# Moving one weight-block issue off ScalarE's queue, and three small reorderings in the head of a layernorm / gated-MLP / state-space kernel

## Chip, cores and metric

The kernel runs on one core of one Trainium2 chip. The metric is the device time of one execution in microseconds (us), as the median of several runs. A run counts as slow when it is over 1.5% above the fastest run of the same kernel; slow runs are named and left out of every comparison.

Engine names in the profile: PE is TensorE's matmuls, PEld its weight loads (they overlap PE: in the kernel before the two are busy for 94% and 47% of the span), DVE is VectorE, ACT is ScalarE, POOL is GpSimd, SP is SyncE. "ACTq" is ScalarE's instruction queue when it issues a DMA. L436 is line 436 of the kernel named; the same statement has another line number in another kernel. Below, "position 15.6" means 15.6 us after the start of the profiled span.

## The reference

The input x has 2048 tokens of 448 columns. It is normalized, and then used twice: by a diagonal complex state-space recurrence, and by a gated MLP of width 1792.

```python
xn = layernorm(x)                                   # x: 1 x 2048 x 448
# A: state-space part, 448 complex states
Lam_bar = exp(dt * Lam);  B_bar = ((Lam_bar - 1) / Lam)[:, None] * Bmat
Bu = einsum("bld,pd->blp", xn, B_bar)               # "projections"
h_t = Lam_bar * h_(t-1) + Bu_t                      # 2048 steps
s = 2 * Re(einsum("blp,dp->bld", h, Cmat)) + xn * Dskip
# B: gated MLP
u = xn @ w_up;  gate = sigmoid(xn @ w_gate)         # 448 x 1792 each
g = silu((gate * u) @ w_down)
return x + s * g
```

## The kernel before

TensorE does all matrix products; VectorE does the scans and half of the evacuations from PSUM; ScalarE does tanh (for the sigmoid), copies and SiLU. A small list scheduler in the Python program decides each engine's order: `add(engine, cost, function, r=reads, w=writes)` records an operation, and the costs serve the ordering alone. `chain=True` keeps operations of one engine in program order.

Only the first 20 us matter here. In this "head" the first four token tiles (128 tokens each) are normalized, transposed on TensorE, and fed to the first three gate column blocks, token by token (`g_head`, 128 columns per matmul). The fourth such step is followed by full gate steps of 512 columns. The normalization of these four tiles needs a square root on ScalarE.

```python
for t in range(4):
    load_x(t, 1, ("SP", "ACT")[t % 2])
load_w("SP", "g", 0, 0)                # (queue, gate/up, row half, block)
load_w("ACT", "g", 1, 0)
...                                    # four short parameter rows
add("ACT", 0.3, lambda: A.preload_act_table_set("sqrt_and_others"), ..., chain=True)
for b in (1, 2):
    load_w("SP", "g", 0, b)
    load_w("ACT", "g", 1, b)           # b == 2: the third block, half of it from ScalarE
load_x(4, 4)
for b in (0, 1):
    load_w("SP", "u", 0, b)
    load_w("SP", "u", 1, b)

def warm_mm(n):                        # matmuls on zeros, to keep TensorE busy
    def f():
        for _ in range(n):
            T.matmul(gu[2][:, 0, :], lhsT=warm[:, 0:P], rhs=warm[:], start=True, stop=True)
    add("PE", 0.43 * n, f, r=["warm"], w=[("gu", 2)])

def chain(t0, n): ...                  # for t0 < 4: sqrt on ACT, then reciprocal on DVE

def pe_transpose(t):                   # xn -> acc (PSUM) -> xnT
    ...
    if t == 0:
        ...                            # 4 blocks copied by ACT, 3 by DVE
    else:
        add("ACT", 0.8, lambda: A.copy(out=xnT[0][:, :, js], in_=tp[:, :, :]), ...)

def tables():                          # sine and cosine tables of the recurrence
    add("ACT", 1.3, lambda: A.preload_act_table_set("silu_and_others"),
        r=["r", "dt", ("xnT", 0, 3, "a")], w=["silutab"])
    ...

warm_mm(9)
for t in range(4):
    stats(t); chain(t, 1); norm(t)
pe_transpose(0); warm_mm(1); pe_transpose(1)
columns(); warm_mm(2); g_head(0, 1)    # columns(): parameter rows to columns
pe_transpose(2); g_head(1, 2)
pe_transpose(3); g_head(2, 3)
...                                    # last 128-column step, then 512-column gate steps
b_load()                               # transposed loads of B, then bT copied by DVE
```

After the head come seven gate and seven up column blocks of 512 tokens for the first chunk. Each gate block is evacuated by a tanh on ScalarE, each up block by a multiply on VectorE. After them come the projections of the state-space part.

Of the kernel before, what the change touches and what calls it, by code (L numbers as in the profile page):

```python
# [14 lines left out]
ACT = mybir.ActivationFunctionType  # L15
# [57 lines left out]
class Plan:  # L73
# [8 lines left out]
    def add(self, eng, cost, fn, r=(), w=(), dma=0, lat=None, chain=False, name=""):  # L82
        o = Op()
        o.idx, o.eng, o.cost, o.fn, o.dma, o.name = len(self.ops), eng, cost, fn, dma, name
        o.lat = LAT.get(eng, 0.0) if lat is None else lat
        o.pre, o.suc = {}, []
        o.start = o.end = None
        for k in r:
            if k in self.w:
                self._edge(self.w[k], o, True)  # L90
        for k in w:
            for q in self.r.get(k, ()):
                self._edge(q, o, False)
            if k in self.w:
                self._edge(self.w[k], o, True)
        for k in w:
            self.w[k] = o
            self.r[k] = []
        for k in r:
            if k not in w:  # L100
                self.r.setdefault(k, []).append(o)
        if chain or eng == "PE":
            key = ("chain", eng)
            if key in self.last_of:
                self._edge(self.last_of[key], o, None)
            self.last_of[key] = o
        self.ops.append(o)
        return o
# [23 lines left out]
    def solve(self, pe_from):  # L132
        t = 0.0
        late = {}
        for o in self.ops:
            if o.eng == "PE":
                t = max(t, pe_from.get(o.name, 0.0))
                late[o.idx] = t
                t += o.cost
        for o in self.ops:  # L140
            o.late = late.get(o.idx, self.horizon)
            for a, kind in o.pre.values():
                a.suc.append((o, kind))
        back = {}
        ready = {}
        for o in self.ops:
            o.left = len(o.suc)

        def release(o):
            end = o.late + o.cost if o.eng == "PE" else min(  # L150
                [self.horizon] + [b.late - self._gap(o, b, k) - self._margin(o, b, k) for b, k in o.suc])
            ready.setdefault(o.eng, []).append((end, o))
        for o in self.ops:
            if not o.left:
                release(o)
        todo = len(self.ops)
        while todo:
            best = None
            for e, lst in ready.items():
                if lst:  # L160
                    t = min(back.get(e, 1e9), max(x[0] for x in lst))
                    if best is None or t > best[0]:
                        best = (t, e)
            t, e = best
            lst = ready[e]
            if e == "PE":
                pick = max(lst, key=lambda x: x[1].idx)
            else:
                pick = max((x for x in lst if x[0] >= t - 1e-9), key=lambda x: (x[0], x[1].idx))
            lst.remove(pick)  # L170
            o = pick[1]
            if e == "NONE":
                o.late = pick[0]
            elif e != "PE":
                o.late = t - o.cost
                back[e] = o.late
            todo -= 1
            for a, kind in o.pre.values():
                a.left -= 1
                if not a.left:  # L180
                    release(a)
        free = {}
        avail = {}
        for o in self.ops:
            o.left = len(o.pre)
            if not o.left:
                avail.setdefault(o.eng, []).append((0.0, o))
        todo = len(self.ops)
        dma_free = {}
        while todo:  # L190
            best = None
            for e, lst in avail.items():
                if lst:
                    s = max(free.get(e, 0.0), min(x[0] for x in lst))
                    if best is None or s < best[0]:
                        best = (s, e)
            s, e = best
            lst = avail[e]
            pick = min((x for x in lst if x[0] <= s + 1e-9), key=lambda x: (x[1].late, x[1].idx))
            lst.remove(pick)  # L200
            o = pick[1]
            o.start, o.end = s, s + o.cost
            free[e] = o.end
            if o.dma:
                if e == "POOL":
                    o.lat = 8.0
                else:
                    q = dma_free[0] = max(dma_free.get(0, 0.0), o.end + 1.2) + o.dma / 280e3
                    o.lat = q + 0.6 - o.end
            todo -= 1  # L210
            for b, kind in o.suc:
                b.left -= 1
                if not b.left:
                    rd = max(a.end + self._gap(a, b, k) for a, k in b.pre.values())
                    avail.setdefault(b.eng, []).append((rd, b))
# [7 lines left out]
def kernel(  # L223
# [18 lines left out]
    V, A, G, T, Q = nc.vector, nc.scalar, nc.gpsimd, nc.tensor, nc.sync  # L242
# [23 lines left out]
    xnT = [flat(t[:], 7, L) for t in xnT_raw]  # L266
# [25 lines left out]
    warm = sbt("warm", [512])  # L292
# [23 lines left out]
    gu = [pp.tile([P, 2, 512], FP32, name=f"gu{i}") for i in range(3)]  # L316
    acc = [pp.tile([P, 512], FP32, name=f"acc{i}") for i in range(2)]

    pl = Plan(185.0)
    add = pl.add  # L320
# [14 lines left out]
    def load_w(eng, k, half, b, r=()):  # L335
        m0, m1 = BLK[k][b]
        ps = slice(half * H, half * H + H)
        c0 = half * 896
        load(eng, [("w", k, half, m) for m in range(m0, m1)], H * 7 * (m1 - m0) * P * 2,
             wgt[k][ps, :, m0 * P:m1 * P],  # L340
             wsrc[k][:, c0 + m0 * P:c0 + m1 * P].rearrange("(s p) f -> p s f", p=H), r=r)

    def tload(keys, o, i, nbytes, r=(), chain=True):
        add("SP", 1.2, lambda: Q.dma_start_transpose(out=o, in_=i), r=r, w=keys, dma=nbytes * 1.5, chain=chain)


    add("DVE", 0.2, lambda: V.memset(warm[:], 0.0), w=["warm"])
    add("POOL", 0.15, lambda: G.memset(ident[:], 0.0), w=["ident"])
    add("POOL", 0.4, lambda: G.affine_select(out=ident[:], in_=ident[:], compare_op=ALU.not_equal, fill=1.0, base=0,
                                             pattern=[[-1, P]], channel_multiplier=1), r=["ident"], w=["ident"])  # L350
# [5 lines left out]
    add("POOL", 0.6, lambda: G.iota(iota[:, 0:NTAB], pattern=[[1, NTAB]], base=0, channel_multiplier=0,  # L356
                                    allow_small_or_imprecise_dtypes=True), w=[("wv", 0)])

    for t in range(4):
        load_x(t, 1, ("SP", "ACT")[t % 2])  # L360
    load_w("SP", "g", 0, 0)
# [1 line left out]
    for k, vec in enumerate((A_log_dt, A_Lambda_im, A_Lambda_re, A_Dskip)):  # L363
        load("ACT" if k < 2 else "SP", ("vrow", k), D * 2, vrow[k:k + 1, :], vec.unsqueeze(0), cost=0.25)
    add("ACT", 0.3, lambda: A.preload_act_table_set("sqrt_and_others"), w=["sqrttab"], lat=1.0, chain=True)
    for b in (1, 2):
        load_w("SP", "g", 0, b)
        load_w("ACT", "g", 1, b)
    load_x(4, 4)
    for b in (0, 1):  # L370
        load_w("SP", "u", 0, b)
# [3 lines left out]
    def warm_mm(n):  # L375
        def f():
            for _ in range(n):
                T.matmul(gu[2][:, 0, :], lhsT=warm[:, 0:P], rhs=warm[:], start=True, stop=True)
        add("PE", 0.43 * n, f, r=["warm"], w=[("gu", 2)])


    def stats(t):
# [47 lines left out]
    def pe_transpose(t):  # L430
        b, a, js = t % NXN, next_acc(), slice(t * P, t * P + P)
        tp = flat(acc[a][:].bitcast(BF16)[:, 0:7 * P], 7, P)

        def f(s0, s1):
            for s in range(s0, s1):
                T.transpose(tp[:, s, :], xn[b][:, s * H:s * H + P], ident[:, :])  # L436
        add("PE", 0.36, lambda: f(0, 6), r=[("xn", b), "ident"], w=[("acc", a)])
        add("PE", 0.06, lambda: f(6, 7), r=[("xnw", b), ("xn", b), "ident", ("acc", a)], w=[("acc", a)])
        if t == 0:
            add("ACT", 0.476, lambda: A.copy(out=xnT[0][:, 0:4, js], in_=tp[:, 0:4, :]),  # L440
                r=[("acc", a)], w=[("xnT", 0, t, "a")])
            add("DVE", 0.27, lambda: V.tensor_copy(out=xnT[0][:, 4:7, js], in_=tp[:, 4:7, :]),
                r=[("acc", a)], w=[("xnT", 0, t, "b")])
        else:
            add("ACT", 0.8, lambda: A.copy(out=xnT[0][:, :, js], in_=tp[:, :, :]),
                r=[("acc", a)], w=[("xnT", 0, t, "a"), ("xnT", 0, t, "b")])

    def dma_transpose(t):
# [60 lines left out]

    def tables():  # L510
        turn = C("turn")
        add("ACT", 1.3, lambda: A.preload_act_table_set("silu_and_others"), r=["r", "dt", ("xnT", 0, 3, "a")], w=["silutab"])
        for pt in range(4):
            vk, nk = ("v", pt), ("nu", pt)
            v, nu = v_t[:, pt, :], nu_t[:, pt, :]
# [2 lines left out]
                r=[("wv", 0), "turn"], w=[vk])  # L518
            add("DVE", 0.4, lambda v=v, nu=nu: V.tensor_single_scalar(out=nu, in_=v, scalar=MAGIC, op=ALU.add),
                r=[vk], w=[nk])  # L520
            add("DVE", 0.6, lambda v=v, nu=nu: V.scalar_tensor_tensor(out=nu, in0=nu, scalar=-MAGIC, in1=v,
                                                                      op0=ALU.add, op1=ALU.subtract),
                r=[vk, nk], w=[nk])
            add("DVE", 0.344, lambda v=v, nu=nu: V.tensor_single_scalar(out=v.bitcast(I32), in_=nu.bitcast(I32),
                                                                        scalar=0x7FFFFFFF, op=ALU.bitwise_and),
                r=[nk], w=[vk])
            so, co = (spm[:, pt, 0, :], cosT[:, pt, :]) if pt < 3 else (cs3[:, 1, :], cs3[:, 0, :])
            add("ACT", 0.537, lambda so=so, nu=nu: A.activation(so, nu[:, 0:L], ACT.Sin, scale=-S),
                r=[nk, "silutab"], w=[("sin", pt)])
# [343 lines left out]
    def g_head(lo, hi):  # L873
        for m in range(3):
            gu_mm(0, "g", m, slots0[m], lo, hi, m == 0)

    pe_transpose(0)
    warm_mm(1)
    pe_transpose(1)
    columns()  # L880
    warm_mm(2)
    g_head(0, 1)
    pe_transpose(2)
    g_head(1, 2)
    pe_transpose(3)
# [139 lines left out]
```

## Time and profile before

The time was 199.57 us (median of 3 runs, 198.74 to 200.06). The profiled run's span was 197.5 us.

The first lines are from the profile's page of the kernel before: busy time of each engine with its share of the span and the number of instructions, and TensorE's granted clock in tenths over 40 equal slices of the span.

```profile
PE 186.0 (94%) x1483; PEld 93.5 (47%) x1490; DVE 161.1 (82%) x278; ACT 87.0 (44%) x122; POOL 36.7 (19%) x90
...
PEclk9959999999999999999999999999999999999999
```

TensorE is busy nearly everywhere. The third digit of the clock, 5, is the one stretch of the head in which half clock is recorded. (Nothing is recorded before 5.48. The nine warm-up matmuls there start 0.43 us apart, eleven matmuls of the same shape at 36.43 take 2.54 us together, and pairs of 512-column matmuls start every 0.22 us at 23 to 24, so the warm-up ran at half that rate too, though its digits say 9.) The table by windows of the kernel before shows it closer. Its columns are the window, its length, then busy time and instruction count of PE, PEld, DVE, ACT and POOL, the granted clock, the mean load of the DMA engines, and GB/s.

```profile
5.00:10.00 5.00, 1.88 (x22) 1.35 (x22) 2.60 (x9) 1.89 (x5) 0.67 (x3) 0.89 0.84 220
10.00:15.00 5.00, 5.00 (x71) 3.85 (x71) 3.92 (x15) 2.95 (x6) 4.53 (x11) 0.50 1.12 231
...
40.00:60.00 20.00, 19.66 (x148) 9.13 (x149) 19.91 (x31) 12.45 (x18) 0.00 (x0) 1.00 0.51 139
60.00:100.00 40.00, 39.41 (x296) 18.88 (x296) 39.31 (x69) 19.41 (x28) 12.24 (x18) 1.00 0.11 24
```

From 40 on, TensorE idles for 0.34 us in 20 and VectorE for 0.09. There, a change to the head cannot make anything shorter; it can only make it start sooner. In the head TensorE idles (1.88 of 5 us busy) and then runs at half clock.

The timeline of the kernel before shows why. Its columns are start, duration, engine, line, operation and operands, count, and in brackets the engine's idle time just before and what ended it.

```profile
3.60 1.28 ACT L365 ACT_TABLE_LOAD   x1 [3.60 <-DMA x_all<-in_A_x_dram]
3.65 3.06 ACTq L326 DMA_DIRECT2D wG<-in_B_w_gate_dram  x2
...
6.82 0.48 ACT L393 ACTIVATE sdb<-mv,epsc 128x1 bf16<-128x1 bf16 x2 [1.94 <-DMA wG<-in_B_w_gate_dram]
7.88 0.56 PE L436 MATMUL acc<-ident,xn 128*128 128x128 bf16 x7 [2.69 <-DVE xn L407]
...
19.96 0.37 PE L647 MATMUL gu<-xnT,wG 64*128 64x512 bf16 x1 [0.88 <-ACT hF L661]
...
21.44 0.37 PE L648 MATMUL gu<-xnT,wG 64*128 64x512 bf16 x1 [0.24 <-issue]
...
26.42 0.38 PE L647 MATMUL gu<-xnT,wU 64*128 64x512 bf16 x1
...
29.57 0.39 DVE L592 COPY bT<-bT 64x896 bf16<-64x896 bf16 x1
...
35.48 0.38 PE L686 MATMUL gu<-xnT,bT 64*128 64x512 bf16 x1
```

ScalarE's table is loaded at 4.88, but its first square root starts at 6.82. The bracket names what it waited for: a gate-weight DMA. ScalarE does not need the data. It is the issue of the third gate block (the second of the two in the ACTq line, 3.06 us together) that goes out only at 6.09, when the first block's transfer has landed (6.07), and in this trace nothing that stands behind it on ScalarE starts before it is out. In the trace the two transfers report their landing on the same semaphore, which may be why the one issue waits for the other transfer. The normalization and the first transpose come behind that, at 7.88. The line at 21.44 matters later: TensorE stopped for a moment and no semaphore explains it ("issue"). The last three lines are the first "up" matmul, the copy of B and the first projection matmul.

### The profile page before, as it was taken

The page shows a single profiled execution, that of the slowest core. Times are in us where ns is not written, and L with a number is a line of the kernel's source. Part 1 is how long each engine was busy: PE and PEld are TensorE (multiplying, and loading weights), DVE is VectorE, ACT ScalarE, POOL GpSimd, SP SyncE. Part 2 cuts the span into 40 slices and gives each one's busy share as a digit, 9 for nine tenths or more (in the row PEclk, how much of TensorE's full clock was granted, in tenths as well). Part 3 has the DMA queues.
Part 4 walks back from the last instruction along what each step waited for, and adds up shares of the span by engine and source line. Part 5 has one row for each costly group of instructions (what it writes and reads, how often), then busy time and mean ns, then how long its engine had stood idle before and what let it go on. Part 6 is the DMA issues. An engine that isn't in the chain of part 4 may idle for free.

```text
span 197.5 us, 3713 instructions
## 1 busy us (share of the span) xinstructions
PE 186.0 (94%) x1483; PEld 93.5 (47%) x1490; DVE 161.1 (82%) x278; ACT 87.0 (44%) x122; POOL 36.7 (19%) x90
## 2 busy tenths in 40 slices
PE   7398999999999999999999999999989999999992
PEld 2277455444445445543445444444435444455561
DVE  3579539699999989999999999999998999630043
ACT  2356898366749573224568221524335331210110
POOL 4186528000004770000257000000000000000000
PEclk9959999999999999999999999999999999999999
DMA  5899957498100014300016410000000000010002
GB/s 159 219 232 225 155 113 97 122 320 226 56 0 0 3 27 91 68 3 0 0 25 89 103 43 3 23 0 27 23 23 0 3 0 25 23 49 24 0 23 71
DMA packets 30025, 13.31 MB, mean 67 GB/s; under 512 B 19636, under 2 KB 30008, under 8 KB 30008
## 3 DMA queue, kind: packets, MB, share of 16 engines
q1 hardware_dynamic: 28324, 12.05, 28.0%
q10 hardware_dynamic: 1684, 1.03, 2.0%
q8 instruction: 11, 0.18, 0.4%
q14 instruction: 6, 0.05, 0.1%
HBM read 6.66 MB, written 1.84 MB: 43 GB/s over the span
## 4 chain that ended last, share of the span: by engine, by line
DVE 48%; PE 35%; issue 6%; POOL 3%; ACT 3%; DMA 2%; SPq 0%; ACTq 0%; DVEq 0%; POOLq 0%
DVE hF L664 10%; PE gu L647 9%; DVE wv L753 8%; PE gu L648 7%; PE acc L837 5%; PE gu L814 5%; PE acc L814 4%; DVE ta L746 3%; DVE tb L747 3%; DVE z L749 3%; DVE hT L770 2%; DMA wG<-in_B_w_gate_dram 2%; DVE ta L767 2%; DVE tb L768 2%; DVE o_t L850 2%
## 5 line engine op out<-in xcount | busy, mean ns | idle before, releaser
L647 PE MATMUL gu<-xnT,wG 64*128 64x512 bf16 (+1 forms) x259 | 48.6, 338 | 1.0 <-ACT hF L661 0.9
L648 PE MATMUL gu<-xnT,wG 64*128 64x512 bf16 (+1 forms) x259 | 48.6, 338 | 0.2 <-issue 0.2
L647 PE MATMUL gu<-xnT,wU 64*128 64x512 bf16 x196 | 46.1, 377 | 0.0
L648 PE MATMUL gu<-xnT,wU 64*128 64x512 bf16 x196 | 46.0, 376 | 0.0
L661 ACT ACTIVATE sig<-gu 128x1024 f32<-128x1024 f32 x21 | 21.4, 1021 | 37.3 <-PE gu L648 37.3
L814 PE MATMUL acc<-wd,hF 128*128 128x448 bf16 x168 | 33.8, 353 | 0.0
L647 PEld LDWEIGHTS <-wG 64*128 64x128 bf16 x259 | 22.4, 101 | 20.2 <-issue 3.1
L814 PEld LDWEIGHTS <-hF 128*128 128x128 bf16 x224 | 21.5, 98 | 21.4 <-issue 2.1
L647 PEld LDWEIGHTS <-wU 64*128 64x128 bf16 x196 | 18.0, 94 | 18.6 <-issue 2.1
L664 DVE SCALAR_TENSOR_TENSOR hF<-sig,gu 128x1024 bf16<-128x1024 f32 x21 | 25.2, 1206 | 0.8 <-PE gu L648 0.8
L837 PE MATMUL acc<-cT,hT 128*128 128x448 bf16 x105 | 24.3, 353 | 0.0
L648 PEld LDWEIGHTS <-wG 64*128 64x128 bf16 x259 | 22.4, 101 | 3.4 <-issue 1.2
L753 DVE TENSOR_TENSOR_SCAN wv<-c_r,st,z 128x512 bf16<-128x512 f32 x18 | 22.8, 1273 | 0.0
L850 DVE TENSOR_TENSOR o_t<-acc,g_t 128x448 bf16<-128x448 f32 x15 | 9.2, 615 | 16.0 <-PE acc L837 16.0
L648 PEld LDWEIGHTS <-wU 64*128 64x128 bf16 x196 | 18.0, 94 | 4.3
L710 ACT CAST bus<-gu 128x1024 bf16<-128x1024 f32 x12 | 12.0, 1009 | 13.2 <-PE gu L699 10.6
L699 PE MATMUL gu<-xnT,bT 128*128 128x512 bf16 x65 | 15.4, 379 | 1.1 <-issue 1.1
L837 PEld LDWEIGHTS <-hT 128*128 128x128 bf16 x119 | 10.4, 98 | 7.3 <-issue 0.4
L398 POOL TENSOR_SCALAR veb<-mv 128x2 bf16<-128x2 bf16 x6 | 3.6, 608 | 52.0 <-DVE st L763 27.6
L820 ACT ACTIVATE g_t<-acc 128x448 bf16<-128x448 f32 x12 | 6.5, 540 | 14.7 <-PE acc L814 14.6
L664 DVE SCALAR_TENSOR_TENSOR hF<-hF,gu 128x1024 bf16<-128x1024 bf16 x7 | 8.5, 1218 | 3.3 <-PE gu L648 3.2
L384 DVE BATCH_NORM_STATS2 bst<-x_all 128x6 f32<-128x448 bf16 x16 | 9.5, 613 | 1.9 <-DMA x_all<-in_A_x_dram 1.9
(130 smaller groups left out, 247.6 us busy)
## 6 DMA issues: line engine op xcount, KB each, us to landing
out_dram<-o_t SPq DMA_DIRECT2D x15, 112.0 KB, 1.7
wd<-in_B_w_down_dram SPq DMA_DIRECT2D x1, 1568.0 KB
x_all<-in_A_x_dram SPq DMA_DIRECT2D x3, 448.0 KB, 4.1
wU<-in_B_w_up_dram SPq DMA_DIRECT2D x2, 448.0 KB, 11.4
wU<-in_B_w_up_dram SPq DMA_DIRECT2D x2, 336.0 KB
wG<-in_B_w_gate_dram SPq DMA_DIRECT2D x2, 224.0 KB, 4.4
wG<-in_B_w_gate_dram ACTq DMA_DIRECT2D x2, 224.0 KB, 4.5
xnT<-xn SPq DMA_TRANSPOSE x24, 2.4
```

The lines of the kernel that those rows point to most:

```text
L384: add("DVE", 0.53, lambda: V.bn_stats(out=bst[b][:], in_=x_all[:, t, :]), r=[("x", t)], w=[("bst", b)])
L647: T.matmul(gu[a][:, 0, ts], lhsT=w_[0:H, s, ms], rhs=x[0:H, s, ts], start=(s == 0), stop=(s == 6))
L648: T.matmul(gu[a][:, 1, ts], lhsT=w_[H:P, (s + 1) % 7, ms], rhs=x[H:P, s, ts], start=(s == 0), stop=(s == 6))
L661: add("ACT", act(1024), lambda: A.activation(th, gu[a][:], ACT.Tanh, scale=0.5), r=[("gu", a)], w=[tk])
L664: add("DVE", dve1(1024), lambda: V.scalar_tensor_tensor(out=ho, in0=th, scalar=1.0, in1=gu[a][:], op0=ALU.add, op1=ALU.mult), r=[("gu", a) ...
L699: T.matmul(gu[a][:, i, :], lhsT=bT[:, kt, i, pt * P:pt * P + P], rhs=x[:, 2 * kt, :], start=False, stop=(kt == 2))
L710: add("ACT", act(1024), lambda u=u, a=a: A.copy(out=bus[u][:], in_=gu[a][:]), r=[("gu", a)], w=[("bus", u)])
L753: dve(1.194, lambda k=k: V.tensor_tensor_scan(out=wv[:, k, :], data0=rb, data1=z[:, k, :], initial=(st[pt][:, k, :] if c else 0.0), op0=AL ...
L814: T.matmul(d, lhsT=hF[c % 2][:, m, h, js], rhs=wd[:, ft, :], start=(ft == 0), stop=(ft == FT - 1))
L820: add("ACT", act(448), lambda: A.activation(g_t[g][:], d, ACT.Silu, scale=0.5), r=[key, "silutab"], w=[("gt", g)])
L837: T.matmul(y, lhsT=hT[c % 2][:, hm, js], rhs=cT[:, cm, c0:c1], start=(i == 0), stop=(i == 6))
L850: add("DVE", dve1(n), lambda od=od, y=y, c0=c0, c1=c1: V.tensor_tensor(out=od, in0=y, in1=g_t[g][:, c0:c1], op=ALU.mult), r=[key, ("gt", g ...
```

## The change

The intent is to start the head earlier and keep it dense:

1. Both halves of the third gate block are issued by SyncE, so that ScalarE's queue does not stop.
2. VectorE, not ScalarE, evacuates the transposed tokens 2 and 3, and ScalarE's last table load no longer waits for token 3.
3. The parameter columns come after the first gate step, and one warm-up matmul goes.
4. Costs that only the planner reads are adjusted.

```diff
-                    q = dma_free[0] = max(dma_free.get(0, 0.0), o.end + 1.2) + o.dma / 280e3
+                    q = dma_free[0] = max(dma_free.get(0, 0.0), o.end + 1.0) + o.dma / 280e3
 ...                                   # other planner costs cut
-    for b in (1, 2):
-        load_w("SP", "g", 0, b)
-        load_w("ACT", "g", 1, b)
+    load_w("SP", "g", 0, 1)
+    load_w("ACT", "g", 1, 1)
+    for h in range(2):
+        load_w("SP", "g", h, 2)
 ...
+        elif t > 1:
+            add("DVE", 0.53, lambda: V.tensor_copy(out=xnT[0][:, :, js], in_=tp[:, :, :]),
+                r=[("acc", a)], w=[("xnT", 0, t, "a"), ("xnT", 0, t, "b")])
 ...
-        add("ACT", 1.3, ...preload_act_table_set("silu_and_others"), r=["r", "dt", ("xnT", 0, 3, "a")], ...)
+        add("ACT", 1.3, ...preload_act_table_set("silu_and_others"), r=["r", "dt", ], ...)
 ...
     pe_transpose(1)
+    warm_mm(1)
+    g_head(0, 1)
     columns()
-    warm_mm(2)
-    g_head(0, 1)
     pe_transpose(2)
```

Compared engine by engine, the built programs differ in order in some twenty rows, nearly all of them in the head.

More of the change, by code (lines that the diff above doesn't have):

```diff
@@ L344, in tload @@
         add("SP", 1.2, lambda: Q.dma_start_transpose(out=o, in_=i), r=r, w=keys, dma=nbytes * 1.5, chain=chain)
-    add("DVE", 0.2, lambda: V.memset(warm[:], 0.0), w=["warm"])
+    add("DVE", 1.0, lambda: V.memset(warm[:], 0.0), w=["warm"])
     add("POOL", 0.15, lambda: G.memset(ident[:], 0.0), w=["ident"])
@@ L357 @@
                                     allow_small_or_imprecise_dtypes=True), w=[("wv", 0)])
+    for e in ("SP", "ACT", "POOL"):
+        add(e, 0.7, lambda: None, chain=True)
     for t in range(4):
@@ L378, in f @@
                 T.matmul(gu[2][:, 0, :], lhsT=warm[:, 0:P], rhs=warm[:], start=True, stop=True)
-        add("PE", 0.43 * n, f, r=["warm"], w=[("gu", 2)])
+        add("PE", (0.43 if n > 1 else 0.22) * n, f, r=["warm"], w=[("gu", 2)])
     def stats(t):
@@ L443, in pe_transpose @@
                 r=[("acc", a)], w=[("xnT", 0, t, "b")])
+        elif t > 1:
+            add("DVE", 0.53, lambda: V.tensor_copy(out=xnT[0][:, :, js], in_=tp[:, :, :]),
+                r=[("acc", a)], w=[("xnT", 0, t, "a"), ("xnT", 0, t, "b")])
         else:
-            add("ACT", 0.8, lambda: A.copy(out=xnT[0][:, :, js], in_=tp[:, :, :]),
+            add("ACT", 0.9, lambda: A.copy(out=xnT[0][:, :, js], in_=tp[:, :, :]),
                 r=[("acc", a)], w=[("xnT", 0, t, "a"), ("xnT", 0, t, "b")])
@@ L511, in tables @@
         turn = C("turn")
-        add("ACT", 1.3, lambda: A.preload_act_table_set("silu_and_others"), r=["r", "dt", ("xnT", 0, 3, "a")], w=["silutab"])
+        add("ACT", 1.3, lambda: A.preload_act_table_set("silu_and_others"), r=["r", "dt", ], w=["silutab"])
         for pt in range(4):
```

## The prediction

> **What bounds the kernel before.** By the table of windows, TensorE is busy 19.66 of 20 us in 40 to 60, 39.41 of 40 in 60 to 100 and 30 of 30 in 150 to 180, and VectorE 109 of 110 us from 40 to 150. The middle can only start earlier; the change touches the first 20 us.
>
> **What holds the head (timeline).** Two variances are ready at 4.6 us and ScalarE's table load ends at 4.88, but its first sqrt starts at 6.82. ScalarE's queue sits until 6.09 before it issues its third gate block, which waits for the first block's transfer (landed 6.07). The first transpose therefore starts at 7.88, after TensorE idled 2.69 us since the warm-up ended at 5.19. The granted clock falls to 0.50 from 8.9 to 15.7 us: pairs of 128-column matmuls start every 107 ns, later every 55 ns. Between the second transpose and the first gate matmuls (9.08 to 10.76) lie a 0.43 us wait, the column matmuls and two warm-up matmuls (1.03 us). At the end of the head the table load (17.59 to 18.88) delays the first tanh, and TensorE waits 0.88 us for its buffer, to 19.96.
>
> **What the change does.** The built programs' orders differ nearly only in the head.
> - ScalarE's blocked issue is gone: the sqrt can start near 4.9, so reciprocal, normalization and transposes come about 1.9 us earlier. TensorE's gap shrinks from 2.7 to about 0.8 us. [...]I expect the clock to stay full; each of three 21-pair stages then takes 1.2 instead of 2.3 us.
> - One warm-up matmul fewer and later columns: about 1 us off the way to the first gate matmuls.
> - VectorE copies tokens 2 and 3 (estimate 0.65 us each, from 0.36 us for 384 columns; ScalarE took 0.91); ScalarE's last table load no longer waits for token 3. But the copy of token 3 stands behind about 2.4 us of sine-table work, costing TensorE perhaps 0.8 us.
>
> Summed in program order, the first full-width gate step starts at about 15.4 instead of 19.96 us, 4.6 us earlier.
>
> **What takes part of it back.** The DMA queue runs full from 9 to 21 us and does not move. The transposed B matrices land near 27 us (one at 26.42). VectorE's copy of B stands after the first "up" evacuation, which moves from 28.3 to about 23; VectorE then idles until about 27, later evacuations are held, and TensorE waits about 1.4 us for a buffer. I expect the state-space projections to start 2.9 us earlier (35.5 to about 32.6), a shift that persists to the end, since nothing later changes in amount.
>
> **Predicted:** 196.7 us, 195.3 to 198.2. Faster by over 2%: 0.10; within 2%: 0.88; slower: 0.02.
>
> **Right or wrong in the profile.** First sqrt near 4.9; first transpose near 6; clock near 1.00 from 5 to 20; first 512-column gate matmul near 15.4; a VectorE idle of 2 to 4 us ending with B's transposes; the first projection matmul near 32.6.
>
> **What would make it wrong.** B landing earlier (gain toward 4.5 us) or later, since SyncE now issues one block more; [...]ScalarE holding buffers; the C matrices' arrival (47 us) becoming a wait.

Two passages are cut from the prediction: its ground for expecting the clock to stay full, and a risk that rested on the same ground. The 1.2 instead of 2.3 us of a 21-pair stage is 21 times the spacing in the trace of the kernel before (55 and 107 ns). In program order the terms came to 4.6 us at the gate step and, less what is taken back, to 2.9 us, from 199.57 to 196.7.

## More of the kernel before

TensorE's waits in the first 40 us of the kernel before (instruction that waited, what ended the wait; total us, times, longest):

```profile
PE acc L436 <- DVE xn L407: 2.7, 1, 2.7
...
PE gu L647 <- ACT hF L661: 0.9, 1, 0.9
...
PE gu L648 <- issue: 0.2, 1, 0.2
```

## The result, and the profile after

The kernel after takes 196.26 us (median of 6 runs, 195.65 to 196.86); the kernel before took 199.71 us in the same rounds (6 runs, 198.74 to 200.06). The ratio is 0.9835, with a 95% interval of 0.9803 to 0.9866: 1.65% faster. Ratios in this text are the mean time of one kernel's fast runs over that of the other's of the same rounds, so they are not quite the ratio of the medians quoted. The profiled span fell from 197.5 to 193.9 us.

The lines of the page of the kernel after that answer to those of before:

```profile
PE 183.2 (94%) x1482; PEld 91.3 (47%) x1489; DVE 161.8 (83%) x280; ACT 85.3 (44%) x120; POOL 38.6 (20%) x90
...
PEclk9999999999999999999999999999999999999999
```

No half clock is recorded in the head any more. The windows of the kernel after:

```profile
5.00:10.00 5.00, 3.69 (x71) 2.75 (x70) 3.90 (x14) 3.67 (x8) 1.59 (x7) 1.00 0.87 218
10.00:15.00 5.00, 4.54 (x137) 4.04 (x135) 4.17 (x11) 2.77 (x6) 3.33 (x8) 1.00 1.11 247
15.00:20.00 5.00, 3.28 (x33) 1.56 (x30) 5.00 (x17) 3.66 (x5) 3.91 (x7) 1.00 1.17 220
...
60.00:100.00 40.00, 39.33 (x303) 18.58 (x302) 39.31 (x68) 18.53 (x25) 13.08 (x20) 1.00 0.11 24
```

TensorE does three times the instructions in 5 to 10 and twice as many in 10 to 15. But in 15 to 20 it is idle for 1.72 us of 5. The middle of the kernel is as dense as before. The timeline of the kernel after shows what those 1.72 us are:

```profile
3.94 0.61 ACTq L326 DMA_DIRECT2D wG<-in_B_w_gate_dram  x1
5.04 0.48 ACT L396 ACTIVATE sdb<-mv,epsc 128x1 bf16<-128x1 bf16 x2
6.10 0.56 PE L439 MATMUL acc<-ident,xn 128*128 128x128 bf16 x7 [0.90 <-DVE xn L410]
...
15.58 0.37 PE L653 MATMUL gu<-xnT,wG 64*128 64x512 bf16 x1 [0.50 <-ACT hF L667]
...
18.05 0.37 PE L653 MATMUL gu<-xnT,wG 64*128 64x512 bf16 x1 [1.22 <-issue]
...
23.01 0.38 PE L653 MATMUL gu<-xnT,wU 64*128 64x512 bf16 x1
...
26.63 0.39 DVE L598 COPY bT<-bT 64x896 bf16<-64x896 bf16 x1 [0.61 <-DMA bT<-in_A_B_im_dram]
...
32.08 0.38 PE L692 MATMUL gu<-xnT,bT 64*128 64x512 bf16 x1
```

ScalarE's queue takes 0.61 us for its one remaining gate issue, and the square root starts at 5.04 instead of 6.82. The first 512-column gate matmul starts at 15.58 instead of 19.96, 4.38 us earlier. Then TensorE stands still for 1.22 us, again for "issue". VectorE's wait for B, which the prediction put at 2 to 4 us, is 0.61 us. TensorE's waits in the first 40 us of the kernel after say the same:

```profile
PE gu L653 <- issue: 1.2, 1, 1.2
...
PE acc L439 <- DVE xn L410: 0.9, 1, 0.9
PE gu L653 <- ACT hF L667: 0.5, 1, 0.5
PE gu L653 <- DVE xnT L448: 0.5, 1, 0.5
```

No wait of TensorE for a buffer that VectorE holds is among them, though the prediction had one of about 1.4 us.

The following table of positions is read from the timelines of the profiled runs. "Stop" is the time from the start of one TensorE matmul to that of the next at the idle called "issue" (so it includes 0.37 us or so of the matmul itself).

| position of | before | after | earlier by |
|---|---|---|---|
| first square root | 6.82 | 5.04 | 1.78 |
| first 512-column gate matmul | 19.96 | 15.58 | 4.38 |
| stop: start to start | 20.82 to 21.44 (0.62) | 16.46 to 18.05 (1.59) | |
| first "up" matmul | 26.42 | 23.01 | 3.41 |
| first projection matmul | 35.48 | 32.08 | 3.40 |
| end of span | 197.55 | 193.88 | 3.67 |

4.38 minus the growth of the stop (1.59 − 0.62 = 0.97) is 3.41, which is what is left at the first "up" matmul. From the projections to the end it takes 162.1 us before and 161.8 after. So the account closes: the gain is made before 15.6, one microsecond is given back at the stop, and the rest reaches the end.

### What the stop is

In every trace in which the stop appears, it comes after exactly 222 recorded TensorE matmuls, whatever these are: in the kernel before, nine matmuls into the first 512-column step, and elsewhere between three (only_warm) and 18 (cold) matmuls in, or still inside the last 128-column step (split4). The page lists eleven transfers of the kind "instruction" on queue q8, 0.18 MB together, so 16 KB each; in split4, whose TensorE has 54 instructions more, it lists twelve. The trace's packet records show one such transfer starting shortly before every stop. TensorE resumes 2.7 to 2.9 us after that transfer's start in all of them:

```
run        transfer starts   222nd matmul starts   next matmul starts   stop   transfer start to resumption
before          18.60              20.82                21.44          0.62             2.84
after           15.19              16.46                18.05          1.59             2.86
only_dma        15.95              17.22                18.68          1.46             2.73
undo_dma        18.76              19.42                21.55          2.13             2.79
only_warm       17.15              17.68                19.89          2.21             2.74
cold            16.72              18.62                19.45          0.83             2.73
split4          13.58              14.33                16.46          2.13             2.88
bt_pool         15.21              16.39                18.06          1.67             2.85
undo_evac       16.92              17.28                19.71          2.43             2.79
undo_pe         14.18              16.45                16.98          0.53             2.80
b_early         15.64              16.37                18.34          1.97             2.70
```

(The other names are the experiments below.) The stop is therefore short when TensorE reaches its 222nd matmul late after the transfer's start (0.53 us when it is 2.27 us after, undo_pe), and long when it reaches it soon (2.21 us when it is 0.53 us after, only_warm). I read it as TensorE waiting for its next instructions; that is a reading: the runs show the count and the transfer, not what TensorE waits for. Beside the stop, the waits of the kernel after over the whole execution list seven idles of TensorE put down to "issue", 1.1 us together and none above 0.2 us, while ten more such transfers of 16,384 bytes start. What makes this one stop long is not shown: TensorE idles for up to 1.91 us at it in a fast run (split4).

### The profile page after: what moved, and what is told of

Read it like the earlier page. It is cut to its first block, busy times and chain, and to the rows that moved or that the text cites. A ratio compares the mean times of both kernels' runs of the same rounds, so it can differ in the third digit from the quotient of the medians.

```text
span 193.9 us, 3710 instructions
## 1 busy us (share of the span) xinstructions
PE 183.2 (94%) x1482; PEld 91.3 (47%) x1489; DVE 161.8 (83%) x280; ACT 85.3 (44%) x120; POOL 38.6 (20%) x90
## 3 DMA queue, kind: packets, MB, share of 16 engines
HBM read 6.66 MB, written 1.84 MB: 44 GB/s over the span
## 4 chain that ended last, share of the span: by engine, by line
DVE 49%; PE 33%; issue 6%; DMA 4%; POOL 3%; ACT 3%; ACTq 0%; DVEq 0%; POOLq 0%
PE gu L653 13%; DVE hF L670 11%; DVE wv L759 9%; PE acc L843 6%; PE gu L820 5%; PE acc L820 4%; DVE ta L752 3%; DVE tb L753 3%; DVE z L755 3%; DMA wG<-in_B_w_gate_dram 2%; DVE hT L776 2%; DVE ta L773 2%; DVE tb L774 2%; DVE o_t L856 2%; DVE wv L791 2%
## 5 line engine op out<-in xcount | busy, mean ns | idle before, releaser
L653 PE MATMUL gu<-xnT,wG 64*128 64x512 bf16 (+1 forms) x259 | 47.1, 324 | 2.7 <-issue 1.2
L654 PE MATMUL gu<-xnT,wG 64*128 64x512 bf16 (+1 forms) x259 | 47.2, 325 | 0.0
L653 PEld LDWEIGHTS <-wG 64*128 64x128 bf16 x259 | 20.8, 94 | 21.7 <-issue 2.5
L654 PEld LDWEIGHTS <-wG 64*128 64x128 bf16 x259 | 20.5, 94 | 2.9 <-issue 2.7
L401 POOL TENSOR_SCALAR veb<-mv 128x2 bf16<-128x2 bf16 x6 | 4.2, 693 | 52.0 <-DVE st L769 27.4
L820 PE MATMUL gu<-wd,hF 128*128 128x448 bf16 x56 | 10.8, 352 | 0.0
```

The source lines that it names most:

```text
L653: T.matmul(gu[a][:, 0, ts], lhsT=w_[0:H, s, ms], rhs=x[0:H, s, ts], start=(s == 0), stop=(s == 6))
L654: T.matmul(gu[a][:, 1, ts], lhsT=w_[H:P, (s + 1) % 7, ms], rhs=x[H:P, s, ts], start=(s == 0), stop=(s == 6))
L820: T.matmul(d, lhsT=hF[c % 2][:, m, h, js], rhs=wd[:, ft, :], start=(ft == 0), stop=(ft == FT - 1))
```

## The experiments

The theories as they stood before the runs:

- **A**, that of the prediction: the blocked issue on ScalarE delays everything and, through TensorE's idle gap, brings the half clock. Taking the issue away makes the gain; the smaller parts add a little.
- **B**, a rival: the gain belongs to the order of the evacuations, of the columns and of the warm-up chain.
- **C**, a rival within A: the price of the blocked issue is the half clock, not the delay itself.
- On what takes part of the gain back: B's late landing (the prediction), or the stop for instructions.

All kernels gave correct results. All ran in three or five rounds (four or six times) beside the kernel before on the same chip; its median there was 199.28 to 199.79 us.

### only_dma: part 1 alone

```diff
  (kernel before)
-    for b in (1, 2):
-        load_w("SP", "g", 0, b)
-        load_w("ACT", "g", 1, b)
+    load_w("SP", "g", 0, 1)
+    load_w("ACT", "g", 1, 1)
+    for h in range(2):
+        load_w("SP", "g", h, 2)
```

> The kernel before with one edit: the third gate block goes out from SyncE twice instead of from SyncE and ScalarE; every other row of every engine's order stays. Theory A (ScalarE's blocked issue was the head's cost, through the late sqrt and the half clock it leads to): first sqrt near 5.0 us, clock 1.00 from 5 to 20 us, first 512-column gate matmul near 15.7, time 2.8 to 3.6 us under before, so nearly the whole gain. Theory B (the gain comes from all three parts about alike, above all from moving the copies and the last table load): sqrt early too, but 1.0 to 1.8 us under before.

Measured: 196.17 us (195.68 to 196.58), ratio 0.9837 [0.9805, 0.9869], against 0.9835 for the whole change. The square root starts at 4.97 and no half clock is recorded. Three lines of its timeline:

```profile
4.97 0.48 ACT L394 ACTIVATE sdb<-mv,epsc 128x1 bf16<-128x1 bf16 x2
...
16.36 0.37 PE L648 MATMUL gu<-xnT,wG 64*128 64x512 bf16 x1 [0.88 <-ACT hF L662]
...
18.68 0.37 PE L649 MATMUL gu<-xnT,wG 64*128 64x512 bf16 x1 [1.08 <-issue]
```

The gate step starts 0.78 us later than in the kernel after (0.88 us of tanh wait against 0.50 is part of it; another part is that this run started slowly: nothing is recorded of its clock before 9.52, and the seven matmuls of its first transpose take 0.93 us instead of 0.56), and the run ends at 194.8 against 193.9 in the profiled runs. Over the runs the two kernels cannot be told apart. One move of one issue gives what can be measured of the gain.

### undo_dma: everything but part 1

```diff
  (kernel after: the four load_w lines put back as they were before)
```

> The changed kernel with the third gate block back on ScalarE's queue. Theory A: sqrt near 6.8 us again, half clock for some us in the head, only about 1 us under before (198.2 to 199.2). Theory B: about 2 us under before.

Measured: 199.13 us (198.11 to 201.89; the run of 201.89 us was a slow one), ratio of fast runs 0.9990 [0.9943, 1.0037]. A half clock is recorded from 8.52 to 11.93, and the square root waits for a gate-weight DMA again:

```profile
7.09 0.48 ACT L395 ACTIVATE sdb<-mv,epsc 128x1 bf16<-128x1 bf16 x2 [2.11 <-DMA wG<-in_B_w_gate_dram]
```

With the blocked issue back, the other three parts are worth nothing that can be measured. They do bring the gate step to 18.55, 1.41 us earlier than before, but the stop is then 2.13 us long instead of 0.62, and the first "up" matmul is at 26.51 against 26.42. Theory B falls with this run and the two below.

### undo_evac and undo_pe: the whole change less part 2, and less part 3

```diff
  undo_evac (kernel after)
-        elif t > 1:
-            add("DVE", 0.53, lambda: V.tensor_copy(...), ...)
-        ... preload_act_table_set("silu_and_others"), r=["r", "dt", ] ...
+        ... preload_act_table_set("silu_and_others"), r=["r", "dt", ("xnT", 0, 3, "a")] ...

  undo_pe (kernel after)
-    warm_mm(1)
-    g_head(0, 1)
     columns()
+    warm_mm(2)
+    g_head(0, 1)
```

> The changed kernel with tokens 2 and 3 copied by ScalarE again and the last table load waiting for token 3 again. Theory A: 0 to 0.6 us over the changed kernel. Theory B: 1 us or more over it.

> The changed kernel with the parameter columns and two warm-up matmuls ahead of the first gate matmuls again. Theory A, and the wait for the second gate block at 8.9 us in the changed kernel's trace: 0 to 0.6 us over the changed kernel, as that wait hides most of the 1 us. Theory B: 0.8 us or more over it.

Measured: undo_evac 196.75 us (195.61 to 199.05), ratio of fast runs 0.9838 [0.9793, 0.9883]. undo_pe 195.94 us (195.4 to 199.44), ratio 0.9801 [0.9756, 0.9845]. Each had one slow run (199.05 and 199.44 us), with a mean granted clock of 0.991 over the run. The profile of undo_evac fell into such a run: it has a half clock from 20.21 to 23.62 after a stop of 2.43 us. So I use none of its later positions. Neither part can be seen in the fast runs; both intervals contain 0.9835.

The profile of undo_pe shows something else, in its timeline:

```profile
16.98 0.37 PE L654 MATMUL gu<-xnT,wG 64*128 64x512 bf16 x1 [0.15 <-issue]
...
26.96 0.39 DVE L598 COPY bT<-bT 64x896 bf16<-64x896 bf16 x1 [1.82 <-DMA bT<-in_A_B_im_dram]
```

Here the stop happens to be short (0.15 us idle), and the wait that the prediction named appears at once: VectorE idles 1.82 us for B, and TensorE then waits for VectorE's buffer before an "up" step and again at the projections (0.77 and 0.76 us from one matmul's start to the next, where about 0.2 is usual between pairs). A microsecond saved at the stop was mostly lost at the next limit: the first projection is at 31.77 against 32.08.

### only_warm: the blocked issue stays, the half clock goes

```diff
  (kernel before, in warm_mm)
-            for _ in range(n):
+            for _ in range(15 if n == 9 else n):
```

The longer first chain fills the idle time before the first transpose (TensorE waits 0.6 us there instead of 2.7), to see whether the granted clock then stays full without the issue being moved.

> The kernel before with 15 instead of 9 warm-up matmuls at the start, all else in place: TensorE then has no gap of 2.7 us before the first transpose, while the sqrt stays late at 6.8 us. It splits theory A: if the half clock is most of the price of the late sqrt, the clock stays at 1.00 and the time falls 1.8 to 2.6 us under before; if the lateness itself is most of it, under 1 us.

Measured: 200.21 us (198.93 to 201.04), ratio 1.0037 [0.9995, 1.0079]: no gain, and perhaps a small loss. The windows of only_warm:

```profile
10.00:15.00 5.00, 5.00 (x136) 4.16 (x136) 3.92 (x15) 4.10 (x7) 4.33 (x11) 1.00 1.11 244
15.00:20.00 5.00, 2.28 (x63) 1.68 (x59) 5.00 (x16) 4.21 (x5) 3.48 (x6) 1.00 1.27 220
20.00:25.00 5.00, 5.00 (x32) 2.30 (x30) 2.85 (x7) 2.10 (x3) 3.44 (x8) 0.66 1.12 144
```

The clock was indeed full where it had been half (1.00 in 10 to 15, with 136 matmuls for 71 before), and the gate step came at 17.46, 2.50 us earlier than before. Then the tanh wait of 0.88 us and the stop of 1.84 us idle left TensorE busy for only 2.28 us of 5, and the clock fell to half from 20.70 to 24.12. Its waits in the first 40 us:

```profile
PE gu L648 <- issue: 1.8, 1, 1.8
...
PE gu L647 <- ACT hF L661: 0.9, 1, 0.9
```

The first "up" matmul came at 27.20, later than before (26.42). Five of six runs had a mean clock of 0.990 or 0.991 over the run; the one at 0.997 took 198.93 us. So removing the half clock alone bought nothing: the time was returned at the stop and in a new half clock. That does not prove that a full clock is worth nothing. It shows that it is worth nothing as long as the rest of the head is late.

### cold: the issue moved, but hardly a warm-up

```diff
  (kernel after, in warm_mm)
-            for _ in range(n):
+            for _ in range(1):
```

> The changed kernel with 1 instead of 9 warm-up matmuls at the start (16 rows fewer for TensorE): the clock should be 0.50 somewhere between 5 and 14 us. If a full clock in the head is worth what the prediction says, this costs 1 to 2.5 us over the changed kernel. Also a test of the 1.2 us stop of TensorE at 16.8 us: if it is the arrival of the next 16 KB of its instructions (a transfer of that size stands just before it in both traces), it comes 16 rows later in the order, after the ninth pair of the first 512-column step instead of the fifth; if it belongs to that step or its data, it stays after the fifth pair.

Measured: 196.72 us (196.0 to 197.5), ratio 0.9868 [0.983, 0.9906]; about 0.5 us more than after by the medians (0.55 more than only_dma, timed in the same rounds), and the intervals overlap. Two lines of its timeline:

```profile
16.88 0.37 PE L653 MATMUL gu<-xnT,wG 64*128 64x512 bf16 x1 [0.50 <-ACT hF L667]
...
19.45 0.37 PE L653 MATMUL gu<-xnT,wG 64*128 64x512 bf16 x1 [0.45 <-issue]
```

The pairs of 128-column matmuls start every 107 ns from 8.59 to 10.30, half the rate of the kernel after (every 55 to 56 ns). The granted clock reads 1.00 in 5 to 10 all the same, because nothing of it is recorded before 10.42; the spacing of the matmuls is what shows the slow start. The gate step comes 1.30 us later than in the kernel after. Most of that is not seen at the end, because the stop is now 0.83 us instead of 1.59: the first projection is at 32.61 against 32.08. The stop comes after the ninth pair of the step, as expected if it goes with the instruction count. With only_warm this answers theory C: the clock without the issue moved gives nothing, and the issue moved with a slow start gives most of the gain.

### split4: the warm-up in four times as many, shorter matmuls

```diff
  (kernel after, in warm_mm)
-            for _ in range(n):
-                T.matmul(gu[2][:, 0, :], lhsT=warm[:, 0:P], rhs=warm[:], ...)
+            for _ in range(4 * n if n == 9 else n):
+                w_ = P if n == 9 else 512
+                T.matmul(gu[2][:, 0, 0:w_], lhsT=warm[:, 0:P], rhs=warm[:, 0:w_], ...)
```

If the stop goes with the count of TensorE's instructions, 27 more of them must bring it 27 matmuls sooner; if it belongs to the place in the program, it stays at the 512-column step.

> The changed kernel with the nine warm-up matmuls of 512 columns split into 36 of 128 columns: the same columns, 54 rows more for TensorE before everything else, all other orders in place. If TensorE's stop at 16.8 us is the arrival of its instructions, it moves 54 rows forward, to about the twelfth pair of the last 128-column stage (near 14.4 us), and there is no stop after the fifth 512-column pair; the time moves by less than 1 us, probably up. If the stop belongs to the step or to its data, it stays after the fifth pair.

Measured: 197.12 us (196.7 to 197.31, 4 runs), ratio 0.9868 [0.9823, 0.9913]. In its timeline the stop has moved into the 128-column step:

```profile
16.46 0.26 PE L655 MATMUL gu<-xnT,wG 64*128 64x128 bf16 x1 [1.91 <-issue]
```

It comes after 222 matmuls again, counted from the start. So it goes with the instruction count; that it is the arrival of instructions is a reading that fits the table above. It is longer here (1.91 us idle) and a half clock is recorded from 15.88 to 19.29.

### bt_pool and b_early: B's copy off VectorE, and B loaded earlier

```diff
  bt_pool (kernel after)
-        add("DVE", 0.53, lambda: V.tensor_copy(out=bT[0:H, 3, :, :], in_=bT[H:P, 3, :, :]), ...)
+        add("POOL", 1.2, lambda: G.tensor_copy(out=bT[0:H, 3, :, :], in_=bT[H:P, 3, :, :]), ...)

  b_early (kernel after)
     for h in range(2): load_w("SP", "u", h, 0)
+    (the four transposed loads of B moved here from b_load)
     for h in range(2): load_w("SP", "u", h, 1)
```

> The changed kernel with the copy of the transposed B matrix on GpSimd instead of VectorE. The prediction said that VectorE's wait for B (0.61 us in the changed kernel's trace) takes back about 1.4 us of the gain by holding TensorE's buffers. The trace of the changed kernel suggests it takes back nothing: then this is the same within 0.3 us. If the prediction was right in that, it is 0.5 us or more faster.

> The changed kernel with the B transposes issued ahead of the second block of up weights. B should land near 22 to 23 us instead of 26.6. Alone it gains at most 0.3 us if the stop at 16.8 us is what sets the pace; if B's arrival takes back 1.4 us as predicted, it gains 0.8 us or more.

Measured: bt_pool 196.46 us (195.99 to 197.41, 4 runs), ratio 0.9844 [0.9795, 0.9893]; b_early 196.56 us (195.6 to 197.26), ratio 0.9844 [0.9805, 0.9884]. Both are as the kernel after. In bt_pool the first projection is at 32.08, the same position as in the kernel after; in b_early B's copy runs at 23.91 instead of 26.63, and the first projection is at 32.52. b_early is the weaker test: its stop is longer (1.97 us), and VectorE waits 2.25 us for B, only earlier, as its timeline shows:

```profile
23.91 0.39 DVE L599 COPY bT<-bT 64x896 bf16<-64x896 bf16 x1 [2.25 <-DMA bT<-in_A_B_im_dram]
```

In the changed kernel, B does not hold the head, and the prediction's account of what takes part of the gain back falls.

### merged: two tokens per gate step, so that the head has fewer instructions

```diff
  (kernel after)
     warm_mm(1)
-    g_head(0, 1)
+    g_head(0, 2)
     columns()
     pe_transpose(2)
-    g_head(1, 2)
```

This has 21 pairs of matmuls fewer, so the 222nd falls far inside the 512-column steps, late after the transfer. The planner also moved some rows of ScalarE and VectorE, so it is not a pure test of the stop.

> The changed kernel with the first gate matmuls of tokens 0 and 1 joined into one stage of 256 columns: the same arithmetic with 84 rows fewer for TensorE ahead of the 512-column steps. The planner moves some rows of VectorE and ScalarE too, so this is a less clean edit than the others. If TensorE's stop is the arrival of its next instructions after a fixed number of rows (row 444 in all traces so far), it comes about 25 pairs into the 512-column steps and is under 0.5 us long, since rows are used up more slowly there; the time then falls by 0 to 1.2 us under the changed kernel, and VectorE's wait for B grows past 1 us. If the stop belongs to the step, it stays after the fifth pair at above 1 us.

Measured: 195.75 us (195.3 to 196.05), ratio 0.9806 [0.9771, 0.9841]. No idle is put down to "issue" before the projections. What is left of the stop is one start after 0.31 us where 0.2 is usual, again at the 222nd matmul, now 52 matmuls into the 512-column steps. The first "up" matmul is at 21.45, 1.56 us earlier than in the kernel after. But the first projection is at 31.61, only 0.47 us earlier. Two lines of its timeline say where the rest went:

```profile
26.88 0.41 DVE L598 COPY bT<-bT 64x896 bf16<-64x896 bf16 x1 [1.40 <-DMA bT<-in_A_B_im_dram]
...
28.59 0.37 PE L653 MATMUL gu<-xnT,wU 64*128 64x512 bf16 x1 [0.92 <-DVE hF L670]
```

This is the wait of the prediction, with nearly its size: VectorE idles 1.40 us for B, and TensorE 0.92 us for the buffer that VectorE then holds.

### merged_be and merged_act: both limits at once

merged_be joins the edits of merged and b_early. merged_act joins merged with B's copy on ScalarE, placed after the second chunk's preparation.

```diff
  merged_act (besides the edit of merged)
-        add("DVE", 0.53, lambda: V.tensor_copy(out=bT[0:H, 3, :, :], ...), ...)      # in b_load()
+        add("ACT", 0.95, lambda: A.copy(out=bT[0:H, 3, :, :], ...), ...)             # in b_fix()
 ...
     prepare(1)
+    b_fix()
```

> Both: the joined stage and B ahead of the second up block. If the stop and B's arrival are two floors of which each hides the other, this gains more than the two alone together: 1.0 to 2.0 us under the changed kernel (194.3 to 195.3), so over 2% under before. If neither is a floor, it is within 0.4 us of the changed kernel.

> The joined stage again, and the copy of the transposed B on ScalarE, behind its four normalizations, so that B's arrival no longer stands in VectorE's way. In the run with the joined stage alone VectorE waited 1.40 us for B and TensorE then 1.07 us for a buffer (start gap 27.3 to 28.59). If B's arrival behind VectorE's queue is the second floor, that gap goes, the first projection matmul comes about 1 us earlier (near 30.6 instead of 31.61), and the time is 194.3 to 195.2, over 2% under before. If something else is the floor (the up weights, the next tokens' transposes), it stays at 195.5 to 196.

Both missed. merged_be took 195.73 us (195.06 to 196.45), ratio 0.9805 [0.9765, 0.9846], the same as merged. B's copy came at 22.40, and the next limit stood behind it: the first projection is at 31.86, and the second half of the "up" weights, which B's loads had pushed back, was late. This wait is in TensorE's waits in the first 40 us of merged_be:

```profile
PE gu L655 <- DMA wU<-in_B_w_up_dram: 0.5, 1, 0.5
```

merged_act took 197.79 us (197.46 to 198.69), ratio 0.9928 [0.9895, 0.9962], slower than merged. GpSimd's timeline in merged_act has the same small operation at very different lengths:

```profile
19.53 4.19 POOL L405 TENSOR_SCALAR nmr<-nmr 128x2 f32<-128x2 f32 x1
...
25.52 0.23 POOL L405 TENSOR_SCALAR nmr<-nmr 128x2 f32<-128x2 f32 x1
```

The chain that normalizes the second chunk goes over GpSimd. Its transposes began at 27.21 instead of 25.07 in merged, the C matrices landed at 49.95 instead of 47.64, and TensorE then waited 0.70 us for ScalarE's evacuation (54.95 to 56.03 from one matmul's start to the next). That this wait is the end of that delay was not tested. During the 4.19 us VectorE ran a series of table operations on 128x513 tiles. Both happened at the same time; no run here shows that one caused the other.

## Why the prediction was right, and where it was wrong

The predicted 196.7 us stands against 196.26 us measured, inside its range. Point by point:

- **ScalarE's blocked issue holds the head: right, and shown.** The first square root is at 5.04 (predicted 4.9), the first transpose at 6.10 (predicted 6), TensorE's gap 0.90 us (predicted 0.8). only_dma gives the gain with this one part, and undo_dma loses it. The table load itself takes 1.28 us in both traces; in the kernel after it ends at 5.02, so the square root now starts when the table is there.
- **The clock stays full: right as a reading, overrated as a cause.** The granted clock is 1.00 from its first record (5.86) to 20, and pairs of 128-column matmuls start every 55 to 56 ns. What brings a half clock is not shown here; the traces give single cases. In the kernel before, one of 6.83 us came after a gap of 2.69 us. In only_warm, with 0.6 us in place of that gap, it did not come there, but two gaps of 0.88 and 1.84 us inside 5 us (TensorE busy 2.28 of 5) were followed by one of 3.42 us; in the kernel after, gaps of 0.50 and 1.22 us (busy 3.28 of 5) were not. And the prediction counted the half clock as a large term ("each of three 21-pair stages then takes 1.2 instead of 2.3 us"). only_warm removed it, moved the gate step 2.50 us forward, and gained nothing at the end; cold had a slow start and lost about 0.5 us; only_dma had one until 9.52 and lost nothing measurable.
- **The gate step at 15.4: right** (15.58).
- **"One warm-up matmul fewer and later columns: about 1 us": a size that leaves no trace in the time.** undo_pe put them back: its gate step was at 15.59, the same position, and its ratio 0.9801. The evacuation on VectorE was sized well in itself (0.65 us estimated, 0.62 and 0.61 measured; the wait behind token 3's copy 0.46 us for 0.8), but undo_evac shows nothing of it in fast runs.
- **What takes part of it back: the failed step.** "VectorE's copy of B stands after the first 'up' evacuation ...; VectorE then idles until about 27, later evacuations are held, and TensorE waits about 1.4 us for a buffer." In the kernel after VectorE waits 0.61 us for B and no wait of TensorE for a buffer that VectorE holds is listed in the first 40 us; bt_pool and b_early change nothing. What took 0.97 us back is the stop after the 222nd matmul. The first "up" evacuation did not reach 23 as predicted but only 24.80, so that B was late by only 0.61 us. The gain predicted at the projections (2.9 us) was 3.40, because 0.97 is less than the predicted loss (4.6 less 2.9, so 1.7 us). That the predicted time came so near is in this part luck: a smaller loss that was not foreseen stood in for a larger one that was.
- **The wait for B is real, but stood behind the stop.** With the stop short (undo_pe) or all but gone (merged), VectorE waits 1.82 and 1.40 us for B. Behind B stand the "up" weights (merged_be). I had named the second limit in line, and had missed the first.
- **The shift persists to the end: right.** From the first projection to the end it takes 161.8 to 162.4 us in every profiled run but one, merged_act (163.9), whose next tokens and C matrices were late.

Is there a faster version? By its median, merged (195.75 us) and merged_be (195.73) are half a microsecond below the kernel after (196.26). They were timed in other rounds, and the intervals of the ratios overlap (0.9771 to 0.9841 against 0.9803 to 0.9866). So no version has been shown to beat it.

What stays open: what decides when the instruction transfer starts (between 1.27 us and 2.22 us before the 222nd matmul in the kernels after and before, and as little as 0.36 us before it in undo_evac); whether the full DMA engines in that stretch (mean load 1.17 in 15 to 20 in the kernel after) make it slow; what brings a half clock; and what held GpSimd in merged_act.

## What to carry to other kernels

Look in a queue that both issues DMAs and computes for an operation that waits for data it does not read: here one issue on ScalarE held the square root for 1.9 us, and moving it to a queue that computes nothing made all of the measurable gain. Before counting the gain of an earlier start, walk forward from it and list the limits that move with it by less or not at all, in order (here the instruction transfer, then B, then the "up" weights). Here the gain ended at the first, 3.41 us being left of 4.38; and removing that one uncovered the next: in merged, 1.56 us gained at the first "up" matmul were 0.47 us at the first projection. Nor was a full clock in one stage worth more than the next waits left of it: only_warm, with the clock full where it had been half, had its gate step 2.50 us earlier and a ratio of 1.0037.
